# A fused attention and feed-forward kernel: steps dealt 4, 9, 9, 8, value products one tick earlier, and a new order of the tail's transfers

## The chip, the cores and the metric

The kernel runs on one core of a Trainium2 chip, in float32. The metric is the device time of one execution in microseconds (us), lower is better. A core has TensorE (PE, matmuls; PEld is its weight load), VectorE (DVE), ScalarE (ACT), GpSimd (POOL) and SyncE (SP). Each of them works through its own instructions in program order and waits on semaphores. SP and POOL also issue transfers (DMA), each in its own queue, in that order.

## What is computed

A gate per token mixes sliding-window attention and a SwiGLU feed-forward layer. S = 2048 tokens, D = 512, 32 heads of 16, a window of 256, hidden size F = 1792.

```python
def reference(A_x, A_wqkv, A_wo, B_x, B_w_gate, B_w_up, B_w_down, gate_w):
    ...
        mask = (idx[:, None] - idx[None, :] >= 0) & (idx[:, None] - idx[None, :] < W)
        scores = jnp.where(mask[None, None], scores, -1e9)
        p = _softmax(scores, axis=-1)
        o = jnp.einsum("bhqk,bhkd->bhqd", p, v)
        return (lambda x, *d: x.transpose(*d))(o, 0, 2, 1, 3).reshape(B, S, D) @ wo
    ...
        g = _silu(x @ w_gate)
        u = x @ w_up
        return (g * u) @ w_down
    x = A_x
    g = _sigmoid((x * gate_w).sum(-1, keepdims=True))
    a = _A_ref(x, A_wqkv, A_wo)
    b = _B_ref(x, B_w_gate, B_w_up, B_w_down)
    return g * a + (1 - g) * b
```

## The kernel before

Products that need precision are made of three matmuls of halves: a value is split into a high part (a rounding copy, a "cast") and a low part (the difference), and high x high, high x low and low x high are added (`split`, L66 to L71; `mm3`, L80 to L82).

**Prologue** (to about 175 us): values, queries and keys, and the gate and up products of the first two of 14 feed-forward units. Results that are needed later go to DRAM: queries and keys to `xd`, values to `vd`, gate and up products to `raws[unit, gate or up, chunk of 512 tokens]`.

**Attention** (to about 639 us). Heads are handled four at a time: G = 8 groups. A group has 16 blocks of 128 tokens (t counts all 128 blocks), and four blocks make a slot, so a group has four slots. A block has four ticks (`hd`), one per head. In a tick stand:
- `stage1(g + 1, i)`: a score matmul for the next group (L554), whose row maxima DVE takes (L556, the instruction `CUSTOM_DVE_ANT_0`, `ISA` in a listing). It writes PSUM tiles `ps1` (two buffers). There is none for the last group's stretch (t >= 112).
- `stage2(g, i)`: a score matmul with the maximum folded in (L593), its exponential on ACT (L595, into `pt`), and after every second head two triangular selects on POOL (L597, L600). It writes `ps2` (two buffers).
- some *steps* of the feed-forward products: a step is a pair of matmuls on the two halves of the array's rows (L498). A unit has 48 steps; ACT copies its results to `ev` tiles (L525, a ring of five buffers that others use too) and they are written to `raws` (L526).
- `tick_end`, which emits everything that a table by tick number (`AT`, filled by `at`, `later`, `spread`) holds for this tick: loads, weight splits, early tiles.

In the first block of each slot the value products of the slot before are added (`av`, 96 small matmuls, L617): 64 for a group's first chunk. They write one `ps1` and one `ps2` tile (two `ps1` tiles in the last group), which `evacuate` empties: ACT copies `ob` (L628), DVE copies `oe` (L634; L630 in the last group), and the sum goes to `od` (L636). Just ahead of `evacuate` the list `UNDER` is emitted (the gate's row sums, L674). After blocks 7 and 15 of a group `put_max` negates and transposes the maxima of half a group (L567, L568) and sends them to the query tiles.

Steps per block: 7 with value products (2, 1, then the products and one more, then 1, 2), else 7 or 8 (`STEPS` = 60 per 8 blocks). So 30 per slot.

In the last group ACT and DVE prepare the start of the feed-forward tail. `tile_early(n)` makes silu of tile n from an exponential on ACT (L711), an addition, a reciprocal and two products on DVE (L712 to L715), and a cast and difference. `INV[c]` (`invert`) loads the denominators of attention chunk c from `od`, inverts them (L689) and writes them to `rd`.

**Tail.** The hidden tiles (c, n), four chunks of 512 tokens by 14 units, are loaded (`load_kept`, L874, tiles `got`, four buffers), multiplied (`hidden`: silu on ACT, L879, product on DVE, L880), split (`halved`: `hh`, `hl`) and multiplied with w_down (`step`, twelve matmuls per tile). Between them stand the output products of attention per chunk: shares of the attention output and of the inverses are loaded by POOL (`load_oc`, `load_rd`, 256 KB each, in the list `shares_due`), divided on DVE (`attn_divide`), split by ACT and POOL (`attn_split`), multiplied (`attn_out`) and added (`attn_put`). A counter m = 14 c + n numbers the tiles. At the end the sums are stored.

## Time and profile before

| what | value |
| --- | --- |
| median of 3 runs | 849.83 us (849.62 to 850.51) |
| the profiled execution | 850.33 us, its span 848.6 us |
| granted TensorE clock, mean of the span | 0.994 |
| longest idle time of PE | 5.48 us before L80, 2.65 us before L593 |
| mean transfer rate | 187 GB/s |

A row of the timeline gives the start and the length in us, the engine, the line, the operation and the tiles (output <- inputs); in square brackets stands how long the engine sat idle before it and what ended that. A row of the waits gives the total in us, the number of times and the longest. A row of the windows gives busy us and count of instructions of PE, PEld, DVE, ACT and POOL, then the granted clock, the share of the 16 DMA engines, and GB/s. A row of a group ends with busy us, the mean ns of one, and the idle time before.

### The profile page before, as it was taken

Reading aid. Unit: us, or ns where it says so; the run is one execution under the profiler, and the core shown is the slowest. Engines: PE = TensorE matmul, PEld = TensorE weight load, DVE = VectorE, ACT = ScalarE, POOL = GpSimd, SP = SyncE. Lnnn points to the kernel's source line nnn. Section 1 sums busy time; section 2 is a strip of 40 time slices with the busy share of each in tenths; the row PEclk is TensorE's granted clock in tenths of the full one; section 3 lists DMA queues with packets and bytes.
Section 4 is the critical chain, followed back from the end, with each engine's and each line's share of the span. In section 5 each row is a group of like instructions: output and inputs, shape, how many; then the busy total and the mean of one; then the engine's idle time right before and its main releaser. Section 6 shows DMA issues by size and latency. Waiting matters only on the chain. (4 is left out here: it accounts for less than half of the span.)

```text
span 848.6 us, 20406 instructions
## 1 busy us (share of the span) xinstructions
PE 826.2 (97%) x7681; PEld 673.8 (79%) x7681; DVE 555.6 (65%) x1420; ACT 471.5 (56%) x955; POOL 395.6 (47%) x708
## 2 busy tenths in 40 slices
PE   8999999999999999999999999999987999999998
PEld 7888888889877787787887878878765878888886
DVE  5675554158886888878878777775474566365552
ACT  7455553211676777667776767767754553444341
POOL 5124440431565666666665665656743433123120
PEclk9999999999999999999999999999998999999999
DMA  8456666485354465644656445524646998586731
GB/s 297 138 173 223 244 252 224 143 282 181 133 166 137 158 212 162 219 159 152 206 166 219 144 141 168 181 85 146 213 146 225 282 264 267 147 248 196 224 118 50
DMA packets 80418, 158.90 MB, mean 187 GB/s; under 512 B 14912, under 2 KB 19392, under 8 KB 80320
## 3 DMA queue, kind: packets, MB, share of 16 engines
q1 hardware_dynamic: 69552, 129.27, 47.3%
q0 software_dynamic: 10192, 27.29, 10.1%
q8 instruction: 60, 0.98, 0.5%
q10 hardware_dynamic: 576, 1.05, 0.4%
q14 instruction: 38, 0.31, 0.1%
HBM read 92.80 MB, written 64.75 MB: 186 GB/s over the span
## 5 line engine op out<-in xcount | busy, mean ns | idle before, releaser
L556 DVE CUSTOM_DVE_ANT_0 ps<-ps,mask 128x384 f32<-128x384 f32 (+2 forms) x512 | 271.3, 544 | 38.0 <-PE ps L554 19.9
L595 ACT ACTIVATE pt<-ps 128x384 f32<-128x384 f32 (+2 forms) x512 | 236.8, 481 | 59.3 <-PE ps L593 24.3
L593 PE MATMUL ps<-q,k 64*128 64x384 f32 (+2 forms) x512 | 175.8, 352 | 4.7 <-ACT pt L595 4.2
L554 PE MATMUL ps<-k,q 63*128 63x384 f32 (+2 forms) x512 | 162.5, 337 | 0.3
L597 POOL TENSOR_SCALAR_AFFINE_SELECT pt<-pt 128x256 f32<-128x256 f32 x256 | 108.6, 424 | 88.7 <-ACT pt L595 87.2
L554 PEld LDWEIGHTS ps<-k,q 63*128 63x128 f32 x512 | 88.8, 184 | 30.2 <-DVE oe L634 10.2
L593 PEld LDWEIGHTS ps<-q,k 64*128 64x128 f32 x512 | 93.8, 185 | 20.9 <-ACT pt L595 16.8
L600 POOL TENSOR_SCALAR_AFFINE_SELECT pt<-pt 128x256 f32<-128x256 f32 x224 | 93.0, 415 | 0.0
L498 PE MATMUL pa<-xhi,wh 64*128 64x512 f32 x368 | 85.8, 405 | 0.0
L498 PE MATMUL pa<-xhi,wl 64*128 64x512 f32 x368 | 85.7, 398 | 0.0
L498 PE MATMUL pb<-xhi,wh 64*128 64x512 f32 x368 | 85.1, 403 | 0.0
L498 PE MATMUL pa<-xlo,wh 64*128 64x512 f32 x368 | 85.1, 398 | 0.0
L498 PE MATMUL pb<-xhi,wl 64*128 64x512 f32 x368 | 83.7, 394 | 0.0
L498 PE MATMUL pb<-xlo,wh 64*128 64x512 f32 x368 | 83.1, 395 | 0.0
L617 PE MATMUL ps<-pt,vg 64*32 64x320 f32 (+4 forms) x2816 | 76.8, 348 | 4.4 <-POOL pt L597 2.9
L880 DVE TENSOR_TENSOR sg<-got,sg 128x512 f32<-128x512 f32 x52 | 43.8, 843 | 54.5 <-ACT sg L879 38.5
L617 PEld LDWEIGHTS ps<-pt,vg 64*32 64x32 f32 x2816 | 53.2, 106 | 30.0 <-issue 8.3
L556 DVE DVE_READ_ACCUMULATOR2_ANT mx<- 128x1 f32 x512 | 72.1, 141 | 0.0
L635 POOL TENSOR_TENSOR oe<-oe,ob 128x512 f32<-128x512 f32 (+1 forms) x28 | 35.2, 1256 | 55.7 <-ACT ob L628 51.1
L68 ACT CAST hh<-sg 128x512 fp32r<-128x512 f32 x53 | 32.7, 616 | 46.4 <-PE ps L81 34.0
L628 ACT COPY ob<-ps 128x512 f32<-128x512 f32 (+1 forms) x32 | 18.3, 573 | 64.1 <-PE ps L617 64.1
L71 POOL TENSOR_TENSOR ol<-raw,oh 128x512 fp32r<-128x512 f32 x16 | 22.1, 1382 | 67.9 <-ACT oh L68 67.8
(248 smaller groups left out, 1805.3 us busy)
## 6 DMA issues: line engine op xcount, KB each, us to landing
got<-raws SPq DMA_DIRECT2D x104, 256.0 KB
raws<-ev SPq DMA_DIRECT2D x96, 256.0 KB
q<-xd SPq DMA_DIRECT2D x96, 128.0 KB
k<-xd SPq DMA_DIRECT2D x96, 128.0 KB
xd<-cx SPq DMA_DIRECT2D x16, 512.0 KB
xd<-cy SPq DMA_DIRECT2D x16, 512.0 KB
od<-oe POOLq DMA_DIRECT2D x32, 256.0 KB, 3.6
raw<-wgu SPq DMA_DIRECT2D x24, 256.0 KB
```

Of the source, the lines that this page charges most:

```text
L68: nc.scalar.copy(hi, src)
L71: lo_eng.tensor_tensor(out=lo, in0=src, in1=hi.bitcast(F32), op=ALU.subtract)
L498: mm = nc.tensor.matmul(ps[me], w[r], x[r], start=not second and i == 0, stop=bool(second) and i == n - 1)
L554: nc.tensor.matmul(ps[:, :n], QT[g % 2][pr][r, q0:q0 + P], KT[g % 2][pr][r, k0:k0 + n], start=True, stop=True)
L556: mx = nc.vector.tensor_tensor_reduce(out=ps[:, :n], in0=ps[:, :n], in1=mask[:, 3 * P - n:], scale=1.0, scalar=NEG, op0=ALU.add, op1=ALU.m ...
L593: nc.tensor.matmul(ps[:, :n], KT[g % 2][pr][r, k0:k0 + P], QT[g % 2][pr][r, k0:k0 + n], start=True, stop=True)
L595: BEHIND.append(nc.scalar.activation(pt[:, j, :n], ps[:, :n], AF.Exp, scale=SCALE))
L597: nc.gpsimd.affine_select(out=pt[:, :, :P], in_=pt[:, :, :P], pattern=[[0, 2], [1, P]], compare_op=ALU.is_ge, fill=0.0, base=0, channel_mu ...
L600: nc.gpsimd.affine_select(out=pt[:, :, 2 * P:], in_=pt[:, :, 2 * P:], pattern=[[0, 2], [-1, P]], compare_op=ALU.is_ge, fill=0.0, base=-1, ...
L617: nc.tensor.matmul(AV[g, c][h][32 * j:32 * j + 32, q0 - c * CH:q1 - c * CH], VG[4 * g + kb // 4][o, kb % 4, 17 * j:17 * j + 32], PT[g, kb, ...
L635: nc.gpsimd.tensor_tensor(out=e[:, lo:], in0=e[:, lo:], in1=o[:, lo:], op=ALU.add)
L880: nc.vector.tensor_tensor(out=sg, in0=gu[1], in1=sg, op=ALU.mult)
```

## The change

1. *Steps.* The blocks of a slot get 4, 9, 9 and 8 steps (`DEAL`), spread evenly over the ticks. The total stays 30.
2. *Value products* with `UNDER` and `evacuate` stand in the first tick of a slot's first block, before that tick's steps, instead of in the second tick after them. `put_max` goes into `UNDER`.
3. *Early tiles.* The two tiles are worked on in parallel, at other ticks: exponential, then DVE's four instructions at once, then the split nine ticks later. Tile 2's raw data are loaded from the first tick of block 14. Tile 3 is no longer loaded in attention, but as the tail's first `got` tile.
4. *Inverses.* Chunks 0 and 1 are inverted in the last group, with twelve ticks between load and reciprocal; chunks 2 and 3 in the tail, by tiles 6, 8 and 10.
5. *Queues.* The last unit's results and five w_down loads go through POOL's queue instead of SP's.
6. *Tail.* The output weights are loaded at tiles 11 to 14 and split at 13 to 16. Shares start at tile 14, one per tile (before: from tile 4, with gaps later). The output products of the four chunks start at m = 22, 31, 42 and 49 (before: 15, 21, 35 and 49). For chunks 0 to 2 ACT now scales the feed-forward sums into one of two buffers, and DVE adds attention's output and stores; before, this held for chunk 0 alone, and in the others the order was reversed.

```diff
+        DEAL = 4, 9, 9, 8
...
-                n = (2, 1, 1, 2)[hd] if values else (k + 1) * STEPS // 32 - k * STEPS // 32
-                if t < G * NB:
-                    run(steps, n)
-                tick_end()
-                if hd == 1 and values:
+                if hd == 0 and values:
                     av(*divmod(d - 1, NCH))
                     while UNDER:
                         UNDER.pop(0)()
                     evacuate(*divmod(d - 1, NCH))
-                    if t < G * NB:
-                        run(steps, STEPS // 8 - 6)
+                if t < G * NB:
+                    n = DEAL[part]
+                    run(steps, (hd + 1) * n // 4 - hd * n // 4)
+                tick_end()
             if i in (7, 15) and g + 1 < G:
-                put_max(g + 1, i // 8)
+                UNDER.append(lambda g=g, i=i: put_max(g + 1, i // 8))
...
-        early = chain(tile_early(0), tile_early(1))
-        for n in range(12):
-            at(4 * (g7 + 10) + 2 + n + n // 6, lambda: run(early, 1))
-        at(4 * (g7 + 12) + 2, lambda: tile_load(2, RAW_AT[2]))
-        at(4 * (g7 + 14) + 2, lambda: tile_load(3, RAW_AT[3]))
+        for n, ticks in enumerate(((2, 5, 5, 5, 5, 14), (7, 14, 14, 14, 14, 23))):
+            early = tile_early(n)
+            for m in ticks:
+                at(4 * (g7 + 10) + m, lambda early=early: run(early, 1))
+        at(4 * (g7 + 14), lambda: tile_load(2, RAW_AT[2]))
...
-        INV = [invert(c) for c in range(NCH)]
-        for c in range(NCH - 1):
+        INV = [invert(c, osb) for c in range(2)]
+        for c in range(2):
             for n in range(2):
-                at(4 * (g7 + 5 + 4 * c) + 2 + 6 * n, lambda c=c: run(INV[c], 1))
+                at(4 * (g7 + 5 + 4 * c) + 3 + 12 * n, lambda c=c: run(INV[c], 1))
...
-            nc.sync.dma_start(WDRAW[f], wd[f])
+            nc.gpsimd.dma_start(WDRAW[f], wd[f])
...
+                        queue = nc.gpsimd if key == UNITS[-1] else nc.sync
+                        later(4 + m, lambda m=m: queue.dma_start(raws[key[1], key[2], 2 * hf + m], places[m]))
...
         run(last_tile)
-        run(INV[3])
...
+            ga = GA[c % 2][:, b]
+            if c < NCH - 1:
+                nc.vector.scalar_tensor_tensor(ga, pa, gate[:, t:t + 1], ga, op0=ALU.mult, op1=ALU.add)
+                nc.gpsimd.dma_start(out[0, t * P:(t + 1) * P], ga)
...
-        loads = seq[4:]
+        loads = seq[3:]
...
+                if n == 6:
+                    inv = [invert(c3, wop) for c3 in range(2, NCH)]
+                    run(inv[0], 1)
+                if n == 8:
+                    run(inv[0])
+                    run(inv[1], 1)
+                if n == 10:
+                    run(inv[1])
             m = NF * c + n
-            if m >= 4 and (m < 20 or (m % 2 == 0 if m < 36 else m % 3 != 2)) and shares_due:
+            if 11 <= m < 15:
+                ready.append(load_wo(m - 11))
+            if 13 <= m < 17:
+                ready.pop(0)()
+            if m >= 14 and shares_due:
                 shares_due.pop(0)()
-            if c == 1:
-                attn_step(0, n - 1)
-            if c > 1 and n == 0:
-                attn_step(c - 1, 7)
-            if c:
-                attn_step(c, n - 7)
+            for o, at_ in enumerate((22, 31, 42, 49)):
+                attn_step(o, m - at_)
```

Three places in the order of instructions. A listing has line, operation, output <- inputs and shape. Line numbers of the changed kernel differ: L556 becomes L566, L567 and L568 become L577 and L578, L634 becomes L644, L595 becomes L605, L628 becomes L638, L689 becomes L457, L880 becomes L872.

DVE around the second slot's value products of group 0 (t = 8), before: two instructions per max (`ISA`), the negation and transpose of `put_max`, the copy `oe` after the products.

```order
L556 ISA ps_2571,mx<-ps_2571,mask 128x384
L556 ISA mx 128x1
L567 TENSOR_SCALAR mt<-mx 128x32
L568 STREAM_TRANSPOSE mtt<-mt 128x32
L556 ISA ps_2592,mx<-ps_2592,mask 128x384
L556 ISA mx 128x1
L556 ISA ps_2605,mx<-ps_2605,mask 128x384
L556 ISA mx 128x1
L634 COPY oe<-ps_2615 128x512
```

The same place in the changed kernel:

```order
L566 ISA ps_2570,mx<-ps_2570,mask 128x384
L566 ISA mx 128x1
L566 ISA ps_2584,mx<-ps_2584,mask 128x384
L566 ISA mx 128x1
L577 TENSOR_SCALAR mt<-mx 128x32
L578 STREAM_TRANSPOSE mtt<-mt 128x32
L644 COPY oe<-ps_2591 128x512
```

One max instead of two now stands between the block's start and the copy, and the pair stands behind it, next to the products.

ACT in the last group, before: tile 0's exponential (L711, `ev<-k_1521`), its cast (L68), tile 1's exponential, the copy `ob` after value products; the rest are the scores' exponentials.

```order
L711 ACTIVATE ev<-k_1521 128x512
L595 ACTIVATE pt<-ps_9919 128x384
L595 ACTIVATE pt<-ps_9922 128x384
L595 ACTIVATE pt<-ps_9942 128x384
L595 ACTIVATE pt<-ps_9945 128x384
L68 CAST k_1507<-ev 128x512
L595 ACTIVATE pt<-ps_9962 128x384
L595 ACTIVATE pt<-ps_9965 128x384
L711 ACTIVATE ev<-q_1505 128x512
L628 COPY ob<-ps_9979 128x512
```

In the changed kernel, from tile 1's exponential on, which now precedes tile 0's cast:

```order
L711 ACTIVATE ev<-q_1505 128x512
L605 ACTIVATE pt<-ps_9960 128x384
L605 ACTIVATE pt<-ps_9963 128x384
L638 COPY ob<-ps_9969 128x512
L605 ACTIVATE pt<-ps_10028 128x384
L605 ACTIVATE pt<-ps_10031 128x384
L605 ACTIVATE pt<-ps_10043 128x384
L605 ACTIVATE pt<-ps_10046 128x384
L605 ACTIVATE pt<-ps_10060 128x384
L605 ACTIVATE pt<-ps_10063 128x384
L68 CAST k_1507<-ev 128x512
```

Between tile 0's exponential and its cast four scores' exponentials stood; now twelve, tile 1's exponential and `ob` do. Tile 1's cast (not shown) stands behind the last scores' exponential.

DVE at the start of the tail, before: the third and fourth inverse (L689), tile 2's product (L724), the last `oe`, then tile 3's product (L880, `sg<-q_1505`) and w_down's differences.

```order
L689 RECIPROCAL den<-den 128x128
L724 TENSOR_TENSOR ev<-k_1521,ev 128x512
L630 TENSOR_TENSOR oe<-ps_10179,ob 128x512
L71 TENSOR_TENSOR k_1507<-ev,k_1507 128x512
L689 RECIPROCAL den<-den 128x128
L880 TENSOR_TENSOR sg<-q_1505,sg 128x512
L71 TENSOR_TENSOR q_1505<-raw,q_1505 128x512
L880 TENSOR_TENSOR sg<-got_10270,sg 128x512
```

In the changed kernel the inverses of chunks 2 and 3 stand here (L872 is the product, `hl` the low half of a tile):

```order
L457 RECIPROCAL den<-den 128x128
L872 TENSOR_TENSOR sg<-got_10345,sg 128x512
L71 TENSOR_TENSOR hl<-sg,hh 128x512
L872 TENSOR_TENSOR sg<-got_10384,sg 128x512
L71 TENSOR_TENSOR hl<-sg,hh 128x512
L457 RECIPROCAL den<-den 128x128
L872 TENSOR_TENSOR sg<-got_10409,sg 128x512
L71 TENSOR_TENSOR hl<-sg,hh 128x512
```

The third moved from ahead of tile 2's product to behind tile 8's, the fourth from ahead of tile 3's to behind tile 10's.

More of the change, by code (lines that the diff above doesn't have):

```diff
@@ L450, in gated_mix, with invert @@
     WD, GOT = {}, {}
+    shares = od.rearrange("g (j e) s -> (g j) e s", e=32)[:, DH]
+    def invert(c, pool):
+        den = pool.tile([P, P], F32, name="den")
+        nc.gpsimd.dma_start(den, shares[:, c * CH:(c + 1) * CH].rearrange("h (q i) -> h q i", q=4))
+        yield
+        nc.vector.reciprocal(den, den)
+        nc.gpsimd.dma_start(rd[c].rearrange("h (q i) -> (h q) i", q=4), den)
+        yield
     def load_wd(f, piece, raw=None):
@@ L525, in copies @@
                         later(1 + m, lambda m=m: nc.scalar.copy(places[m], ps[m]))
-                        later(4 + m, lambda m=m: nc.sync.dma_start(raws[key[1], key[2], 2 * hf + m], places[m]))
+                        queue = nc.gpsimd if key == UNITS[-1] else nc.sync
+                        later(4 + m, lambda m=m: queue.dma_start(raws[key[1], key[2], 2 * hf + m], places[m]))
                 return copies
@@ L681, in gate_end @@
             nc.vector.tensor_scalar(igate, gate, -1.0, 1.0, op0=ALU.mult, op1=ALU.add)
-        shares = od.rearrange("g (j e) s -> (g j) e s", e=32)[:, DH]
-        def invert(c):
-            den = osb.tile([P, P], F32, name="den")
-            nc.gpsimd.dma_start(den, shares[:, c * CH:(c + 1) * CH].rearrange("h (q i) -> h q i", q=4))
-            yield
-            nc.vector.reciprocal(den, den)
-            nc.gpsimd.dma_start(rd[c].rearrange("h (q i) -> (h q) i", q=4), den)
-            yield
         def wd_early(k, f, piece):
             at(k, lambda: later(4, load_wd(f, pieces[piece], kept())))
-        RAW_AT, TILE_AT = (14, 8, 14, 8), (12, 10, 13)
+        RAW_AT, TILE_AT = (14, 8, 14), (12, 10, 13)
         TILE = [None] * 3
@@ L826, in load_oc @@
             nc.gpsimd.dma_start(OC[c][:, k], heads[:, :DH, c * CH:(c + 1) * CH])
-        RD = [t.bitcast(F32) for c in range(2, 4) for t in (xhi[c], xlo[c])]
+        RD = [t.bitcast(F32) for t in (xhi[2], xlo[2], xhi[3], xhi[2])]
         def load_rd(c, k):
@@ L887, in halved @@
             return c, n, hh, hl
-        ACC, GA = {}, []
+        ACC, GA = {}, [by_k(slot("k11", F32)), const.tile([P, NK, CH], F32, name="xlo3")]
         COLS = slice(0, D // 2), slice(D // 2, D)
@@ L925, in gated_mix @@
         seq = [(c, n) for c in range(NCH) for n in range(NF)]
-        ready = [load_wo(k) for k in range(3)]
-        GOT[0, 3] = GOT[3]
+        ready = []
         shares_due = [lambda f=f, c=c, k=k: f(c, k) for c in range(NCH) for k in range(NK) for f in (load_oc, load_rd)]
-        loads = seq[4:]
+        loads = seq[3:]
         for _ in range(3):
```

23 lines of the change are left out of this document (3 added, 20 removed).

## The prediction

> **What bounds the kernel now.** I read the page's busy times first, then the waits of TensorE (PE), then windows set at the starts of the value products and at the gaps, then the timeline inside the two worst gaps.
>
> ```profile
> PE 826.2 (97%) x7681; PEld 673.8 (79%) x7681; DVE 555.6 (65%) x1420; ACT 471.5 (56%) x955; POOL 395.6 (47%) x708
> ```
>
> PE is the bound, and no part of the change takes a matmul away, so only PE's idle and slow stretches can be won. The waits of PE over the whole run name five:
>
> ```profile
> PE ps L80 <- ACT hh L68: 5.5, 1, 5.5
> PE ps L593 <- ACT pt L595: 4.2, 3, 2.6
> PE ps L617 <- POOL pt L597: 2.9, 4, 0.7
> PE ps L617 <- DVE mx L556: 1.4, 3, 0.5
> PE ps L82 <- DVE hl L71: 1.2, 1, 1.2
> ```
>
> The windows show where they fall (after the engines' busy times stand the granted clock, the DMA share and GB/s):
>
> ```profile
> 490.20:542.10 51.90, 51.39 (x721) 41.69 (x720) 40.08 (x137) 36.14 (x80) 33.65 (x72) 1.00 0.45 147
> 594.50:606.00 11.50, 11.50 (x141) 9.08 (x140) 5.32 (x10) 7.79 (x19) 8.85 (x17) 1.00 0.58 185
> 618.60:636.20 17.60, 13.41 (x165) 10.52 (x164) 12.66 (x11) 9.00 (x23) 7.59 (x17) 0.90 0.49 157
> 626.40:630.10 3.70, 3.70 (x21) 3.70 (x22) 3.63 (x3) 1.74 (x4) 2.42 (x7) 0.54 0.60 224
> 647.20:652.60 5.40, 0.00 (x0) 0.00 (x0) 2.08 (x3) 0.64 (x2) 0.54 (x1) 0.81 0.59 221
> 652.60:657.50 4.90, 4.75 (x11) 3.35 (x12) 4.90 (x10) 4.22 (x8) 4.89 (x9) 0.51 0.66 189
> 657.50:688.50 31.00, 31.00 (x137) 25.32 (x135) 16.19 (x25) 17.20 (x30) 11.67 (x15) 1.00 1.06 279
> 689.80:845.10 155.30, 154.86 (x685) 128.16 (x685) 82.94 (x110) 59.90 (x105) 37.85 (x45) 1.00 0.62 185
> ```
>
> A slot of the last group (four blocks and one set of value products) takes 11.5 us undisturbed and 17.6 us in 618.6 to 636.2, where PE idles 4.2 us and then runs 3.7 us at a granted clock of 0.54. From 647.2 it idles 5.4 us and runs the next 4.9 us at 0.51. From 689.8 to 845.1 nothing is left to win. So the change can win in three places: the transition between attention and the feed-forward tail, the waits before value products, and small waits inside the slots that busy time hides.
>
> **The early tiles (attention's last slot).** The timeline of ACT, DVE and PE ahead of the 2.65 us gap:
>
> ```profile
> 617.54 0.94 DVE L689 RECIPROCAL den<-den 128x128 f32<-128x128 f32 x1
> 618.41 3.29 DVE L713 RECIPROCAL ev<-ev 128x512 f32<-128x512 f32 x1
> 622.46 0.69 DVE L715 TENSOR_TENSOR ev<-k,ev 128x512 f32<-128x512 f32 x1
> 623.18 0.62 ACT L68 CAST k<-ev 128x512 fp32r<-128x512 f32 x1 [5.69 <-DVE ev L715]
> 624.24 0.82 PE L593 MATMUL ps<-q,k 64*128 64x384 f32 x2 [2.65 <-ACT pt L595]
> ```
>
> The cast of tile 0 stands on ACT five ticks after its exponential, with DVE's chain of 3.29 + 2 x 0.69 us and an inverse of 0.94 us between. ACT waits 5.69 us in it, and the exponentials of the scores behind it release PE's score buffers. After the change the cast stands nine ticks after DVE's chain was issued, across a set of value products: nine ticks at 11.5/16 = 0.72 us are 6.5 us, where the chain needs about 5 (an addition, 3.29, and two of 0.69). Tile 1's cast moves behind the last exponential, so that its wait (I estimate about 1 us, since the low half of tile 0 goes ahead of its chain) has only copies and the third tile behind it, and no score buffer hangs on those. Removed: 17.60 - 13.41 = 4.2 us of idle, and of the slow 3.7 us the share 1 - 0.54, 1.7 us. Against it I set 1.0 us for remaining ACT waits, because the last blocks have ever fewer columns and give PE less cover. **Term: -4.9 us.** Bounds: -5.9 (no wait left) and 0 (rival 3). The two inverses of the denominators that stay here each cost DVE 0.94 us beside a free PE: nothing; uncovered, 1.9 us.
>
> **The start of the tail.**
>
> ```profile
> 641.47 4.04 SPq L874 DMA_DIRECT2D got<-raws  x8
> 645.54 0.63 ACT L879 ACTIVATE sg<-got 128x512 f32<-128x512 f32 x1 [4.44 <-DMA got<-raws]
> 645.13 0.54 POOL L687 DMA_DIRECT2D den<-od  x1 [4.17 <-DMA od<-oe]
> 650.43 0.95 DVE L689 RECIPROCAL den<-den 128x128 f32<-128x128 f32 x1 [9.72 <-DMA den<-od]
> 651.30 0.63 DVE L880 TENSOR_TENSOR sg<-q,sg 128x512 f32<-128x512 f32 x1
> 651.96 0.62 ACT L68 CAST hh<-sg 128x512 fp32r<-128x512 f32 x1 [5.79 <-DVE sg L880]
> 652.63 0.80 PE L80 MATMUL ps<-q,hh 128*128 128x512 f32 x1 [5.48 <-ACT hh L68]
> ```
>
> DVE stands 9.72 us in the fourth inverse, whose load had to wait for the last attention output to land; tile 3's product stands behind it, and PE idles 5.48 us. The change moves the inverses of chunks 2 and 3 behind tiles 8 and 10. That removes 5.48 us and the slow stretch after it, 4.9 x (1 - 0.51) = 2.4 us. The 1.23 us before 689.8 (the L82 row of the waits) lies at the end of the 31 us in which DMA was saturated (share 1.06, 279 GB/s); the change takes ten-odd loads of 256 KB out of that stretch, so I count it as removed. Together -9.1 us.
>
> What it adds there: tile 3 is no longer loaded under attention; it is now the first `got` load. Today's first one was issued at 641.47, after SyncE had stood behind unit 13's writes and two w_down loads, which move to POOL's queue; so it should go out when the value products release the memory, 2.8 us earlier against PE. Its tile is needed three tiles after them. A tile is twelve matmuls of 0.227 us (31.00/137 in the saturated window), 2.7 us, so 8.2 us after. The load lands 4.1 us after issue (641.47 to 645.54), the next pair about 2 us later at 279 GB/s (512 KB), and silu 0.63, product 0.63, cast 0.62 and low half 0.7 follow, part of them behind the next tile's silu: 7 to 8.5 us. It is a close fit. A second close fit is the fourth inverse: its load goes out only after the third's store, and DVE may stand some 3 us in it, but DVE is then up to three tiles (8.2 us) ahead. A third: from tile 14 one share of 256 KB is issued per tile beside 512 KB of `got`, 768 KB in 2.7 us or 289 GB/s, over the 279 measured, for the eleven tiles before output products stretch the steps: 31.0 us of transfers in 29.9 us of PE, plus four weights of 256 KB; four buffers of lead hide most of it. For the three I set 2.0 us. **Term: -7.1 us**, bounds -9.1 and 0.
>
> POOL's queue takes nine more transfers of 256 KB at 0.54 us each (the 645.13 row), 5 us of POOL, which is 47% busy and whose selects for the last products are already ahead of most of them: nothing; if they stood ahead of all, the last value products would wait at most 1.6 us for the three that come early. The evacuation of chunks 1 and 2 goes from DVE to ACT, four of about 0.63 us, 2.5 us per chunk boundary on an engine that is busy 59.90 of the last 155.30 us: nothing; uncovered, 2 x 2.5 us.
>
> **The maxima (put_max).** Timeline of DVE, with PE's next value product:
>
> ```profile
> 397.00 0.37 DVE L567 TENSOR_SCALAR mt<-mx 128x32 fp32r<-128x32 f32 x1
> 397.41 0.21 DVE L568 STREAM_TRANSPOSE mtt<-mt 128x32 f32<-128x32 f32 x1
> 397.55 0.53 DVE L556 CUSTOM_DVE_ANT_0 ps<-ps,mask 128x384 f32<-128x384 f32 x1
> 398.28 0.51 PE L617 MATMUL ps<-pt,vg 64*32 64x320 f32 x8 [0.46 <-DVE mx L556]
> 398.50 0.92 DVE L674 SCALAR_TENSOR_TENSOR xn<-xn,gwb 128x512 f32<-128x512 f32 x1
> 400.90 0.69 DVE L634 COPY oe<-ps 128x512 f32<-128x512 f32 x1 [1.47 <-issue]
> 401.51 0.56 DVE L556 CUSTOM_DVE_ANT_0 ps<-ps,mask 128x384 f32<-128x384 f32 x1
> ```
>
> Negation and transpose hold the next block's first max back, and the value product waits for the buffer which that max frees. The seven waits of L617 in the list above are this pattern: 2.9 + 1.4 = 4.3 us. Under the product DVE has 1.47 us idle, and the pair needs about 0.6 to 0.9: covered. **Term: -4.3 us**, bounds -4.3 and 0 (the wait moves to the copy behind it).
>
> **The deal.** PE's work per slot is the same: 30 steps, 16 pairs of score matmuls, one set of value products. The rows that give their pace:
>
> ```profile
> 402.57 0.40 PE L498 MATMUL pb<-xlo,wh 64*128 64x512 f32 x2
> 402.80 0.40 PE L498 MATMUL pb<-xhi,wl 64*128 64x512 f32 x2
> 403.04 0.34 PE L554 MATMUL ps<-k,q 63*128 63x384 f32 x1
> 403.21 0.40 PE L498 MATMUL pb<-xhi,wh 64*128 64x512 f32 x2
> 411.69 2.56 PE L617 MATMUL ps<-pt,vg 64*32 64x320 f32 x96
> ```
>
> A step is 0.23 us, a pair of scores 0.17, the products 2.5: 30 x 0.23 + 16 x 0.17 + 2.5 = 12.1 us, against 51.9/4 = 13.0 per slot, so about 0.9 us per slot is lost in short waits. In the three blocks without products PE now has 23 steps (7.3 us); a tick is about 0.6 us, and two buffers ask for one max (0.34 of matmul, 0.57 of max) per two ticks, so they lose little. With 26 steps (8.0 us) they should lose less: I take 0.2 us per slot of gain. In the block with products the steps fall from 7 to 4. The products now follow the first scores directly: the last max before them ends 0.34 + 0.57 after its scores began, and PE is there after two steps and a pair, 0.17 + 0.46 + 0.17 = 0.80, so it waits 0.1 to 0.2. After them PE has a single step per tick (0.40 us) where copy and maxes follow each other at 0.6: by the order of 400.90 and 401.51 the third and fourth scores and the next block's first wait some 0.45 us together, against 0.15 to 0.3 today. Gain and loss are equal to a tenth. **Term: 0**, bounds over 28 slots -5.6 (0.2 each, no new wait) and +8.4 (0.3 each).
>
> **Sum.** -4.9 - 7.1 - 4.3 + 0 = -16.3 us. The profiled execution's span is 848.6 us, its own time 850.33, the median of the runs 849.83: the median lies 1.2 above the span. 848.6 - 16.3 + 1.2 = 833.5.
>
> The slow clock is a term that rests on a row: 0.54 came after an idle time of 2.65 us. [...]
>
> **Rivals.**
> 1. *The first tiles come late.* If tile 3's load takes the place of the inverse (landings 2 us apart and the next tile's silu ahead of its cast), PE idles some 3 us and the clock falls again for 2.4 us, and tile 4 and 5 wait 1 to 2 us more: +6, 839.5. For it: the saturated DMA rows; against: SyncE's queue is free.
> 2. *The deal's wait decides, and the kernel is slower.* The products now begin 0.8 us closer to the last exponentials, and need the selects of the last block near their end:
>
> ```profile
> PEld ps L617 <- POOL pt L597: 6.4, 11, 1.1
> ```
>
>    This wait exists already, up to 1.1 us. If every slot had it, the 28 slots would cost 28 x 1.1 = 31 us, and with it 864. It decides from 16.3/28 = 0.58 us per slot. Against it: the last block's probabilities are used in the products' last third, 1.7 us after their start.
> 3. *The change doesn't do what it says for the early tiles:* the cast still stands on DVE, the 2.65 us gap and its slow clock stay: +4.9, 838.4.
> 4. *Better:* the deal also wins its 5.6 and the three close fits cost nothing: 833.5 - 5.6 - 3 = 825.
>
> **How the numbers follow.** Forecast (829 to 837) 0.54; rival 1 0.15; rival 2 0.16, of which 0.04 lies below today's time (a wait of 0.2 to 0.5 per slot, 839 to 848); rival 3 0.05; rival 4 0.10. About 0.2% (1.7 us) is what a measurement of this kernel tells from no change. Slower by more than that is rival 2 beyond 0.64 us per slot, 0.09; within it, 0.03; faster 0.88. The range from 825 to 845 leaves out the far half of rival 2 and a corner of rival 4.
>
> **What would show it.** Right: no PE gap over 1.5 us between 600 and 690, granted clock 1.00 there, the last three slots of attention each 11 to 12 us, no wait of ACT for L715's successor over 2 us, DVE's waits for `den` without PE idle behind them, and four slots of a group in 51 to 52 us. Wrong in the deal: a group of over 52.5 us, with PE's waits at the first or the last value products. Wrong in the tail: a PE wait on `hh` or `hl` of tiles 3 to 6 or at tiles 20 to 25. The whole is wrong if rival 2's wait stands in most slots.

## The result, and the profile after

The changed kernel takes 847.52 us (median of 19 runs, 844.67 to 849.72); the kernel before took 849.83 in 19 runs beside it (848.55 to 853.08). The ratio is 0.9968, interval 0.9958 to 0.9978. It is faster, but by 2.3 us where 16.3 were forecast, and outside the range. The profiled execution has a span of 846.7 us and a time of its own of 848.42. One execution of e5 below, 1310 us at a granted clock of 0.56, is left out of its times and ratio.

The busy times of the changed kernel, and its list of PE's waits (who was waited for, total us, times, longest):

```profile
PE 829.8 (98%) x7681; PEld 680.0 (80%) x7681; DVE 558.7 (66%) x1420; ACT 472.6 (56%) x955; POOL 400.3 (47%) x717
```

```profile
PE ps L82 <- DVE hl L71: 4.4, 3, 3.6
PE ps L627 <- DVE mx L566: 1.5, 9, 0.2
PE ps L603 <- ACT pt L605: 1.4, 4, 0.7
...
PE ps L80 <- ACT ob L638: 0.9, 1, 0.9
```

Four of the five waits that the prediction named went down: 5.5 us on `hh` (gone), 4.2 on the exponentials (now 1.4), and the two ahead of the value products, 4.3 together (now 1.5). The fifth, on `hl`, went up from 1.2 to 4.4 us. Together they fall from 15.2 to 7.3 us. Yet PE's busy time rose from 826.2 to 829.8 us with the same 7681 matmuls. Time that vanished as waits came back inside "busy", where a list of waits doesn't show it.

To see where, cut the run at the start of the last stage-1 score and at the start and end of the last group's value products. The rows of the line of the stage-1 scores give the first (shortest, median and longest duration in ns, then first and last start in us): L554 of the kernel before, and the same line of the changed kernel:

```profile
L554 PE MATMUL ps<-k,q x512: 219/337/447, 172.6 to 580.1; 63*128 63x384 f32 x150, 63*128 63x128 f32 x11, 63*128 63x256 f32 x10
```

```profile
L564 PE MATMUL ps<-k,q x512: 218/337/447, 172.7 to 585.3; 63*128 63x384 f32 x150, 63*128 63x128 f32 x11, 63*128 63x256 f32 x10
```

The scores start together and end 5.2 us later than before: a stretch that was forecast to shrink by 4.3 us (the maxima) grew. Worked out from the starts and ends of single rows:

| stage (us) | before | forecast | changed | e1 | e9 |
|---|---|---|---|---|---|
| first score of group 1 to the last stage-1 score | 364.3 | 360.0 | 369.4 | 359.1 | 359.1 |
| last group: from its first value products (those of the group before) to the end of its last | 56.9 | 52.0 | 51.9 | 50.4 | 50.3 |
| tail: from there to the end | 209.9 | 202.8 | 208.4 | 205.2 | 202.7 |
| span | 848.6 | 832.3 | 846.7 | 832.0 | 829.4 |

(The rest of a span is some 216 us ahead of the first stage, and 1.1 to 1.8 between the first and the second.) e1 and e9 are kernels of the experiments. Three stages, three answers: the stage of the early tiles came out as forecast, the tail won 1.4 us of 7.1, and the body of attention lost 5.1 us where it should have won 4.3. One caution on the second row: the change moves the products one tick forward, and with them the start of this stage. From the last stage-1 score to the end of the last products it is 58.7 us before, 53.0 in the changed kernel and 52.2 in e1.

Windows of the changed kernel at the last group, and at the one large gap in the tail:

```profile
586.40:638.30 51.90, 50.46 (x752) 39.70 (x751) 26.41 (x37) 35.63 (x84) 34.64 (x76) 1.00 0.54 175
676.50:680.10 3.60, 0.05 (x1) 0.05 (x1) 3.60 (x2) 0.70 (x2) 3.48 (x4) 1.00 0.68 211
681.50:684.90 3.40, 3.40 (x9) 2.62 (x9) 0.12 (x1) 2.52 (x5) 0.00 (x0) 0.50 0.52 154
```

The last line of the three comes behind the one above it: 1.45 us after PE's 3.58 us of idle time, which end at 680.05, the granted clock falls to 0.50 for 3.4 us.

The timelines of DVE, POOL and ACT of the changed kernel ahead of that gap tell what PE waited for:

```profile
665.88 0.95 DVE L457 RECIPROCAL den<-den 128x128 f32<-128x128 f32 x1 [5.51 <-DMA den<-od]
...
674.61 1.36 DVE L872 TENSOR_TENSOR sg<-got,sg 128x512 f32<-128x512 f32 x1 [4.23 <-ACT sg L871]
675.90 4.10 DVE L71 TENSOR_TENSOR hl<-sg,hh 128x512 fp32r<-128x512 f32 x1
...
661.16 0.54 POOL L455 DMA_DIRECT2D den<-od  x1 [2.30 <-DMA rd<-den]
667.12 0.54 POOL L458 DMA_DIRECT2D rd<-den  x1 [5.42 <-DVE den L457]
667.66 1.60 POOL L811 DMA_DIRECT2D raw<-wo  x3
674.13 1.30 POOL L71 TENSOR_TENSOR wol<-raw,woh 128x512 fp32r<-128x512 f32 x1 [4.87 <-ACT woh L68]
...
676.30 1.27 POOL L71 TENSOR_TENSOR wol<-raw,woh 128x512 fp32r<-128x512 f32 x1
677.51 0.63 POOL L823 DMA_DIRECT2D xhi<-od  x1
678.17 1.27 POOL L71 TENSOR_TENSOR wol<-raw,woh 128x512 fp32r<-128x512 f32 x1
...
673.42 0.62 ACT L68 CAST woh<-raw 128x512 fp32r<-128x512 f32 x1 [4.14 <-DMA got<-raws]
```

Read it from the top. The fourth inverse's load goes out at 661.16, when the third's store has landed, because both use the one `den` buffer. DVE stands 5.51 us for it. POOL stands behind DVE, for the store at 667.12, and the three loads of `wo` are queued behind that store. ACT comes to the first cast of `wo` (L68, `woh`) and stands 4.14 us; the profile names a tile's load (`got`), but the first `wo` load landed at 673.28, 5.6 us after its issue and just before the cast. When it ends, POOL makes its low halves one after the other, and in their midst DVE's `hl`, which takes 0.68 us elsewhere, takes 4.10. PE's tile waits for that `hl`. So PE idles some 10 us after the inverse, through five links. Two of them are read from the order in the queues, and the experiments below test the first and the last.

### The profile page after: what moved, and what is told of

Read it like the earlier page. It is cut to its first block, busy times and chain, and to the rows that moved or that the text cites. A ratio compares the mean times of both kernels' runs of the same rounds, so it can differ in the third digit from the quotient of the medians.

```text
span 846.7 us, 20416 instructions
## 1 busy us (share of the span) xinstructions
PE 829.8 (98%) x7681; PEld 680.0 (80%) x7681; DVE 558.7 (66%) x1420; ACT 472.6 (56%) x955; POOL 400.3 (47%) x717
## 4 chain that ended last, share of the span: by engine, by line
PE 85%; DMA 6%; DVE 3%; ACT 2%; POOL 1%; issue 1%; SPq 0%; DVEq 0%; ACTq 0%
PE pb L507 14%; PE pa L507 14%; PE ps L627 9%; PE ps L564 7%; PE ps L380 6%; PE ps L603 5%; PE pb L380 4%; PE pa L380 4%; PE ps L82 4%; PE ps L81 4%; PE ps L80 4%; PE ps L211 3%; DMA got<-raws 2%; PE pb L81 2%; PE pb L80 2%; DMA xhi<-rd 2%
## 5 line engine op out<-in xcount | busy, mean ns | idle before, releaser
L566 DVE CUSTOM_DVE_ANT_0 ps<-ps,mask 128x384 f32<-128x384 f32 (+2 forms) x512 | 272.7, 544 | 50.5 <-PE ps L564 28.6
L605 ACT ACTIVATE pt<-ps 128x384 f32<-128x384 f32 (+2 forms) x512 | 236.0, 479 | 67.1 <-PE ps L603 30.0
L603 PE MATMUL ps<-q,k 64*128 64x384 f32 (+2 forms) x512 | 173.8, 349 | 2.2 <-ACT pt L605 1.4
L607 POOL TENSOR_SCALAR_AFFINE_SELECT pt<-pt 128x256 f32<-128x256 f32 x256 | 106.1, 416 | 73.6 <-ACT pt L605 73.1
L627 PE MATMUL ps<-pt,vg 64*32 64x320 f32 (+4 forms) x2816 | 78.7, 348 | 3.0 <-DVE mx L566 1.5
L627 PEld LDWEIGHTS ps<-pt,vg 64*32 64x32 f32 x2816 | 56.7, 106 | 25.6 <-issue 10.2
L872 DVE TENSOR_TENSOR sg<-got,sg 128x512 f32<-128x512 f32 x53 | 43.4, 818 | 45.3 <-ACT sg L871 36.6
L566 DVE DVE_READ_ACCUMULATOR2_ANT mx<- 128x1 f32 x512 | 72.4, 141 | 0.0
L68 ACT CAST hh<-sg 128x512 fp32r<-128x512 f32 x53 | 32.6, 615 | 43.6 <-PE ps L81 38.2
L71 DVE TENSOR_TENSOR hl<-sg,hh 128x512 fp32r<-128x512 f32 x53 | 40.6, 766 | 22.9 <-ACT hh L68 22.9
L71 POOL TENSOR_TENSOR ol<-raw,oh 128x512 fp32r<-128x512 f32 x16 | 25.3, 1578 | 60.2 <-ACT oh L68 60.2
```

Of the source, the lines that this page charges most:

```text
L71: lo_eng.tensor_tensor(out=lo, in0=src, in1=hi.bitcast(F32), op=ALU.subtract)
L566: mx = nc.vector.tensor_tensor_reduce(out=ps[:, :n], in0=ps[:, :n], in1=mask[:, 3 * P - n:], scale=1.0, scalar=NEG, op0=ALU.add, op1=ALU.m ...
L603: nc.tensor.matmul(ps[:, :n], KT[g % 2][pr][r, k0:k0 + P], QT[g % 2][pr][r, k0:k0 + n], start=True, stop=True)
L605: BEHIND.append(nc.scalar.activation(pt[:, j, :n], ps[:, :n], AF.Exp, scale=SCALE))
L607: nc.gpsimd.affine_select(out=pt[:, :, :P], in_=pt[:, :, :P], pattern=[[0, 2], [1, P]], compare_op=ALU.is_ge, fill=0.0, base=0, channel_mu ...
L627: nc.tensor.matmul(AV[g, c][h][32 * j:32 * j + 32, q0 - c * CH:q1 - c * CH], VG[4 * g + kb // 4][o, kb % 4, 17 * j:17 * j + 32], PT[g, kb, ...
```

## The experiments

Ratios are to the kernel before, run beside it on the same chip. Two things have to be told apart: which of three edits lengthened the body (the deal, the place of the products, the maxima under them), and which link of the chain in the tail decides.

**e1, e2, e3: the deal and the place, one by one.** e1 puts both back as they were and keeps all else; e2 keeps the new deal with the products behind the second scores; e3 keeps the products behind the first scores with the old steps. e1's edit:

```diff
-                if hd == 0 and values:
+                n = (2, 1, 1, 2)[hd] if values else (k + 1) * 60 // 32 - k * 60 // 32
+                if t < G * NB:
+                    run(steps, n)
+                tick_end()
+                if hd == 1 and values:
                     av(*divmod(d - 1, NCH))
...
                     evacuate(*divmod(d - 1, NCH))
-                if t < G * NB:
-                    n = DEAL[part]
-                    run(steps, (hd + 1) * n // 4 - hd * n // 4)
-                tick_end()
+                    if t < G * NB:
+                        run(steps, 1)
```

e2 only moves the block with `av` and `evacuate` behind `tick_end()` with `hd == 1`; e3 only takes e1's `n` in place of DEAL, with the extra step at the end of the second tick.

> The changed kernel with the steps and the place of the value products as before (7, then 8, 7, 8 or 7, 8; products in the second tick), and put_max still under the products. The body of attention is read from the start of the last of the 512 stage-1 scores: 580.1 us before, 585.3 us in the changed kernel. Theory A (the deal and the place together cost the body some 9 us, and put_max under the products wins its 4.3 us): 575.8 us, and the whole 838 us. Rival B (put_max under the products wins nothing, since its wait only moves behind the copy of the products): 580 us, 842 us. Rival C (the body's loss comes from transfers or from elsewhere in the change): 585 us and no change of time.

> The changed kernel with the products back in the second tick after its steps, but the steps dealt 4, 9, 9, 8. If the short deal costs (one step per tick in the block with products, so that scores wait in turn for copy and maxima), the last stage-1 score starts at 583 us or later, and the kernel takes 845 us or more. If the place costs (products that begin before the last tick's maximum, exponential and selects are done), it starts at 576 to 578 us, and the kernel takes about 839 us.

> The changed kernel with the products in the first tick as in the change, but seven steps in that block (2, 2, 1, 2 after the products) and 8, 7, 8 or 7, 8 in the others. If the place costs: last stage-1 score at 583 us or later, 845 us or more. If the short deal costs: 576 to 578 us, about 839 us. If both are needed for the loss, this and the kernel with the new deal and the late products both stand near 580 us.

| | time, us | ratio | last score starts | block with products | second | third | fourth | slot |
|---|---|---|---|---|---|---|---|---|
| before | 849.46 | 1 | 580.1 | 5.41 | 2.54 | 2.60 | 2.56 | 13.11 |
| e1: old steps, old place | 833.84 | 0.982 [0.9802, 0.9839] | 574.5 | 5.24 | 2.55 | 2.59 | 2.56 | 12.93 |
| e2: new deal | 842.12 | 0.9916 [0.9897, 0.9935] | 582.1 | 4.97 | 2.86 | 2.79 | 2.58 | 13.20 |
| e3: new place | 840.04 | 0.9884 [0.9863, 0.9905] | 578.8 | 5.33 | 2.58 | 2.61 | 2.57 | 13.09 |
| changed: both | 847.52 | 0.9968 [0.9958, 0.9978] | 585.3 | 4.97 | 2.94 | 2.82 | 2.58 | 13.31 |

(The last five columns are the mean lengths of the four blocks of a slot, from score row to score row, over groups 1 to 5.) The deal alone ends attention's scores 7.6 us later than e1, the place alone 4.3, both 10.8. Up to 0.5 us of that lies ahead of group 1's first score, where these kernels do not differ; counted from there it is 7.4, 4.1 and 10.3. So each costs by itself, and the two nearly add up; of the expected cases the last of e3's (both kernels near 580 us) is the nearest. e1 is some 4 us faster than expected; its scores end 1.3 us earlier, and its tail takes 205.2 us instead of 208.4 (its fourth inverse stood 1.27 us). Rival B of e1, that the maxima under the products win nothing, is refuted: they stand there in e1 too, and its body is the shortest of the five.

The table also says how. A step is 0.23 us of PE. The deal takes three steps out of the block with products, 0.70 us, and that block gets 0.27 shorter. The three arrive in the second and third block, which had 8 and 7 and now have 9 each, and these get 0.31 + 0.20 = 0.51 us longer. Where steps arrive, most of their price is paid; where they left, a wait takes most of their room. Most of this wait is hidden from the list of PE's waits (6.5 us on `oe` stand there in e2, none in e1, e3 and the changed kernel), since a matmul's record (0.34 to 0.40 us) is longer than the 0.17 to 0.23 us after which the next one starts in the prediction's rows (402.57 to 402.80, 403.04 to 403.21). The waits of the weight loads (PEld), which stand ahead of the matmuls (in the changed kernel the last one starts at 585.1 us, its matmul at 585.3), show it. Between 216 and 574 us, e1:

```profile
PEld ps L564 <- DVE oe L644: 10.2, 27, 0.4
...
PEld ps L564 <- DVE mx L566: 6.5, 31, 0.3
PEld ps L627 <- issue: 4.5, 16, 0.3
```

e2, the new deal in the old place:

```profile
PEld ps L564 <- DVE oe L644: 16.2, 26, 0.7
PEld ps L564 <- DVE mx L566: 11.7, 58, 0.4
PEld ps L627 <- POOL pt L607: 6.3, 17, 0.5
```

e3, the old steps in the new place:

```profile
PEld ps L564 <- DVE mx L566: 12.8, 63, 0.3
PEld ps L627 <- issue: 9.6, 24, 0.5
```

In e2 no step is left between the products and the next scores, which need the buffer that DVE's copy `oe` frees: the waits for it grow from 0.38 us each (27 of them) to 0.62 (26). The new place trades this wait for more, shorter ones on the maxima (31 waits become 63) and a later start of the products. These waits can't be added up to the loss, because part of each lies beside the matmul ahead (over the changed kernel's span PEld is busy 80% and PE 98%).

PE's timeline of one such block in the changed kernel, and DVE's beside it:

```profile
453.38 2.55 PE L627 MATMUL ps<-pt,vg 64*32 64x320 f32 x96
455.87 0.50 PE L507 MATMUL pb<-xhi,wh 64*128 64x512 f32 x2
...
456.76 0.44 PE L564 MATMUL ps<-k,q 63*128 63x384 f32 x1
...
457.29 0.44 PE L564 MATMUL ps<-k,q 63*128 63x384 f32 x1
...
457.92 0.44 PE L564 MATMUL ps<-k,q 63*128 63x384 f32 x1
...
456.01 0.69 DVE L644 COPY oe<-ps 128x512 f32<-128x512 f32 x1 [0.77 <-PE ps L627]
456.62 0.56 DVE L566 CUSTOM_DVE_ANT_0 ps<-ps,mask 128x384 f32<-128x384 f32 x1
...
457.24 0.57 DVE L566 CUSTOM_DVE_ANT_0 ps<-ps,mask 128x384 f32<-128x384 f32 x1
...
457.76 0.57 DVE L566 CUSTOM_DVE_ANT_0 ps<-ps,mask 128x384 f32<-128x384 f32 x1
```

After the products scores start every 0.53 to 0.63 us, at the pace of copy and maxima on DVE; with one step per tick PE has 0.23 + 0.17 = 0.40 us of work in between. That is the floor of the block: fewer steps there leave holes.

**e6: the gentlest deal.** On e5 (below), steps 6, 8, 8, 8 with the products behind the second scores, to see whether a flat deal wins where 4, 9, 9, 8 loses.

```diff
-                n = (2, 1, 1, 2)[hd] if values else (k + 1) * 60 // 32 - k * 60 // 32
+                n = (2, 1, 1, 2)[hd] if part == 0 else 2
...
-                    if t < G * NB:
-                        run(steps, 1)
```

> The same with the steps dealt 6, 8, 8, 8, products in the second tick. Theory (the block with products takes what DVE and ACT need, some 4.9 to 5 us, however few steps it has; a block with 8 steps is already paced by PE, and only blocks with 7 lose): the block with products falls from 5.24 to about 5.1 us, the others stand at 2.57, a slot wins 0.1 us, the last stage-1 score starts 3 us earlier, near 571.5 us, and the kernel takes about 3 us less than the one with the old deal. Rival (every step taken out of that block costs): the last score starts at 574 us or later.

It takes 832.47 us, ratio 0.9797 [0.9777, 0.9818], where e5 beside it has 0.9792; its last score starts at 575.7, and its blocks are 5.22, 2.54, 2.63 and 2.55. The expected 3 us are not there: the rival's sign (574 us or later) came. The step more in the third block costs 0.04 us, so there was room; but the step less in the block with products saves only 0.02. It is the one right behind the products, and the wait on the copy shows it (weight loads of e6, same stretch):

```profile
PEld ps L564 <- DVE oe L644: 16.3, 27, 0.7
```

So the block with products stands close to its floor with 7 steps already (a step less saves 0.02 us of 0.23, three less in e2 0.27 of 0.70), and neither deal beats e1's 12.93 us per slot.

**e7: the maxima alone.** e1 with put_max called where the kernel before calls it:

```diff
-                UNDER.append(lambda g=g, i=i: put_max(g + 1, i // 8))
+                put_max(g + 1, i // 8)
```

> The kernel with the old deal and place (833.8 us, last stage-1 score at 574.5 us), with put_max back ahead of the next block's maxima. Theory (its negation and transpose hold the products' buffer): seven gaps of PE of 0.4 to 0.7 us ahead of value products return, last score at 579 to 580 us, 838 to 839 us. Rival (the gain of that kernel over the first came from elsewhere): last score at 575 us and no change of time.

840.84 us, 0.9901 [0.9877, 0.9924]. The last score starts at 580.1, 5.6 us after e1's as the theory had it, and the wait list has the old pattern back:

```profile
PE ps L627 <- POOL pt L607: 2.9, 4, 0.7
...
PE ps L627 <- DVE mx L566: 1.4, 3, 0.5
```

Those are the seven waits of the prediction to the digit, and the blocks are those of the kernel before (5.41, 2.54, 2.60, 2.56). From group 1's first score on, the maxima are worth 5.2 us (364.3 against 359.1). The time is 2 us over what was expected, because 2.6 us of e7's longer span are in the tail: its fourth inverse stood 4.48 us (1.27 in e1) and a `hl` took 4.1 us, although the tail's code is the same. In e3 a `hl` took 4.1 us too, and in e1 the longest took 2.3. So the collision depends on how the engines stand to each other when the tail begins; what shifts them was not looked for.

**e4: a second den buffer.** The changed kernel with two buffers and both inverses' loads issued together, at tile 6 (the two edits were not tried apart):

```diff
-    def invert(c, pool):
-        den = pool.tile([P, P], F32, name="den")
+    def invert(c, pool, n=1):
+        den = pool.tile([P, P], F32, name="den", bufs=n)
...
-                    inv = [invert(c3, wop) for c3 in range(2, NCH)]
+                    inv = [invert(c3, wop, 2) for c3 in range(2, NCH)]
...
+                    run(inv[1], 1)
...
-                    run(inv[1], 1)
```

> The changed kernel with two buffers for the denominators of chunks 2 and 3 and both loads issued at tile 6. In the changed kernel DVE stands 5.51 us in the fourth inverse; POOL issues the output weights only behind its store, ACT stands 4.14 us in their cast, DVE's low half takes 4.10 us beside two low halves of weights on POOL, PE idles 3.58 us and runs 4.9 us at a granted clock of 0.65. Theory A (the late inverse starts that chain): the wait of DVE falls under 1 us, the PE gap goes with its slow clock, 5 to 6 us less, 842 us. Rival B (the low halves of the output weights on POOL hold DVE wherever they stand): the inverse's wait goes, a DVE instruction of 3 us or more beside them stays, and PE keeps a gap over 2 us: at most 1 us less.

842.08 us, 0.9909 [0.9892, 0.9925]; the tail takes 202.2 us, 6.3 less than in the changed kernel and 7.7 less than before. That is the expected 5 to 6 us and a little more. DVE's inverses now wait for nothing, and a window on the place of the old gap is full:

```profile
657.27 0.94 DVE L457 RECIPROCAL den<-den 128x128 f32<-128x128 f32 x1
...
660.48 0.95 DVE L457 RECIPROCAL den<-den 128x128 f32<-128x128 f32 x1
```

```profile
660.00:690.00 30.00, 30.00 (x134) 24.85 (x133) 17.26 (x24) 16.89 (x30) 13.78 (x19) 1.00 0.84 250
```

**e8: the last link alone.** The changed kernel with the low halves of `wo` on DVE; the single `den` buffer stays.

```diff
-            return lambda: split(woh[:, k], wol[:, k], raw, *act)
+            return lambda: split(woh[:, k], wol[:, k], raw, nc.scalar, nc.vector)
```

> The changed kernel with the low halves of the output weights on DVE instead of POOL. In the changed kernel DVE's low half of a tile takes 4.10 us where others take 0.68, beside two of POOL's low halves and two of its transfers; PE idles 3.58 us behind it. Theory A (POOL at work on SBUF holds DVE's instruction): no low half over 1.5 us at tiles 13 to 16, the gap of 3.58 us falls under 1.5 us, 3 to 5 us less, though the inverse's wait of 5.5 us stays. Theory B (the late inverse alone took DVE's lead): the gap stays over 2.5 us.

844.44 us in its one run, span 842.7, tail 204.6; a single run, so its time is only an indication. DVE's queue of e8:

```profile
665.13 0.95 DVE L457 RECIPROCAL den<-den 128x128 f32<-128x128 f32 x1 [4.95 <-DMA den<-od]
...
675.86 0.68 DVE L71 TENSOR_TENSOR hl<-sg,hh 128x512 fp32r<-128x512 f32 x1
676.47 0.68 DVE L71 TENSOR_TENSOR wol<-raw,woh 128x512 fp32r<-128x512 f32 x1
```

The inverse still stands 4.95 us, and yet the gap at 676 is gone: no `hl` from 660 to 684 us takes more than 0.69 us. Of the 6.3 us that the chain costs, 3.8 hang on its last link, by this run. Part of the rest stands in new gaps of 0.27, 1.13 and 0.61 us between 692 and 700, the three waits of this row of e8:

```profile
PE ps L82 <- DVE hl L71: 2.0, 3, 1.1
```

**e5 and e9: the best parts together.** One wait is left between attention and the tail of e1: PE waits 2.18 us for the last `ob` there, 0.89 in the changed kernel. ACT's queue of e1 around it:

```profile
626.48 0.62 ACT L68 CAST q<-ev 128x512 fp32r<-128x512 f32 x1 [2.80 <-DVE ev L715]
627.11 1.28 ACT L723 ACT_TABLE_LOAD   x1
628.41 0.63 ACT L723 ACTIVATE ev<-k 128x512 f32<-128x512 f32 x1
628.94 1.05 ACT L534 COPY ev<-pb 128x512 f32<-128x512 f32 x2
629.89 0.60 ACT L638 COPY ob<-ps 128x512 f32<-128x512 f32 x1
```

The cast of tile 1 stands 2.80 us, and `ob` behind it frees a `ps` buffer that PE's first tile waits for (the 2.18 us). e5 is e1 with e4's pair of buffers and this cast behind `ob`; e9 is the same kernel once more, and the readings below are of its trace.

```diff
-        for n, ticks in enumerate(((2, 5, 5, 5, 5, 14), (7, 14, 14, 14, 14, 23))):
+        for n, ticks in enumerate(((2, 5, 5, 5, 5, 14), (7, 14, 14, 14, 14, 26))):
```

> The kernel with the old deal and place and put_max under the products (833.8 us), with both denominator loads issued together, and the cast of early tile 1 moved behind the copy ob of the last value products. There ACT stood 2.80 us in that cast ahead of ob, PE idled 2.18 us for ob and ran 3.4 us at a granted clock of 0.50. Theory: that gap, its 1.7 us of slow clock and the inverse's wait of 1.27 us go, and with them most of the gap of 0.72 us: 829 to 830 us. Rival: the table load and silu of tile 2, which stay ahead of ob, keep PE waiting over 1 us: 832 us.

> The kernel of e5 once more (old steps, products behind the second scores, maxima under them, two den buffers, tile 1's cast behind ob), for a profile of it. Theory: 831 to 832.5 us, last scores of attention starting near 574.5, no idle time of TensorE over 1.3 us between 625 and 720 and the granted clock 1.0 there, tail (end of the last value products to the end) near 202.5. Rival: taking tile 1's cast back only moves the wait to a later tile: an idle time of 2 us or more stands at 628 to 645 as in e1, and the time is over 833.

e5 gave a ratio of 0.9792 [0.9774, 0.9809] (three runs, 830.71 to 832.22, all above what was expected), e9 a median of 830.05 us (829.69 to 832.59) and 0.9771 [0.9747, 0.9795], 1 us under what was expected of it. e5's times alone would have spoken for its rival (832 us); e9's trace shows that the rival's wait of PE, over 1 us for `ob`, is not there. The busy times of e9 and its largest wait of PE:

```profile
PE 821.0 (99%) x7681; PEld 667.6 (80%) x7681; DVE 555.7 (67%) x1420; ACT 471.8 (57%) x955; POOL 403.2 (49%) x717
```

```profile
PE ps L82 <- DVE hl L71: 1.5, 2, 1.4
```

Its last score starts at 574.6. PE's busy time is down to 821.0 us for the same 7681 matmuls, the wait on `ob` is gone, the tail takes 202.7 us, and one gap over 0.4 us is left after attention, 1.37 at 689.5 (no more than 1.3 was expected). It is another wait: DVE's division of attention's output, ahead of that `hl`, stood 6.42 us for a share to land. This kernel is faster than the one before and than the changed one.

**e10: e9 with e8's edit.**

> e9 with the low halves of the output weights on VectorE instead of GpSimd, as in e8. If GpSimd's two low halves in a row cost TensorE time here too, 829.5 to 831, some 1 us under e9. Rival: with both den buffers VectorE is ahead enough to take a long low half without TensorE feeling it, and the four halves added to VectorE's queue cost as much as they save: within 0.7 us of e9, either way.

830.37 us, 0.9767 [0.9742, 0.9791]: no different from e9. The rival holds. With both buffers the low halves of `wo` on GpSimd (657 to 663 us in e9) meet no `hl` that PE waits for.

## Why the prediction was wrong, step by step

- **The early tiles, -4.9.** Right in kind, and the fit of the number (5.0 in the table) is partly luck. In e1, with the old deal and place, the stretch from the last stage-1 score on is 6.5 us shorter than before, beyond the bound of 5.9; in the changed kernel the deal and the place take 0.8 of that back, and the rest is the shifted start of the stage. One sentence behind the term was wrong, that behind tile 1's cast "no score buffer hangs on those": `ob` frees a `ps` buffer that the first tile waits for. The cast waited 2.39 us for an estimated 1. PE paid 0.89 us for it, counted in the tail, and in e1 2.18 us, with a granted clock of 0.50 for 3.4 us after it.
- **The start of the tail, -7.1.** The bound of 0 was nearer (-1.4). The pieces named as close fits were looked at one by one: the first `got` load was in time, and the shares cost 0.37 us (DVE stood 3.54 us for one at 704.9). The 279 GB/s that the third close fit took for the most that the transfers move was no ceiling: from 638.3 to 660.0 the changed kernel moves 334 GB/s. The fourth inverse was the one that failed, and not as feared. DVE's stand (5.51 us for an estimated 3) was covered but for 0.50 us, as the text said. What it left out is who else stands behind that wait: POOL's store, behind it POOL's `wo` loads, behind these a cast on ACT. The mechanism that should win was right and its size nearly so: with the second buffer the tail wins 7.7 us.
- **The maxima, -4.3.** Right in kind, 5.2 in size (e7 against e1), beyond the bound of 4.3. The seven visible waits are the 4.3; the other 0.9 us were not looked for further.
- **The deal and the place, 0.** This is the step that failed, by 10.3 us in the body and 0.8 in the last group (e1 against the changed kernel). With the 5.7 missing in the tail, and less the 0.9 and 1.6 that the maxima and the early tiles won beyond their terms, that is 14.3 of the 14.4 us by which the span missed. The sentence is "Gain and loss are equal to a tenth." The gain of 0.2 us per slot in the blocks without products was right: three steps arrive for 0.51 us instead of 0.70. The loss was not: three steps leave the block with products and 0.43 of their 0.70 us stay behind as waits, and the new place costs a further 0.11. The prediction's own rows gave 0.1 to 0.2 ahead of the products and 0.15 to 0.3 more behind them, against a gain of 0.2, so 0.05 to 0.3 per slot; it took the end of that range which is nearest to nothing. Measured are 0.38 per slot (13.31 against 12.93), above even its bound of 0.3.
- **The rivals.** What came is nearest to the second, which named the deal as what decides: 0.38 us per slot, below the 0.58 from which it turns the sign. Its chance was set too low (0.04 for "a wait of 0.2 to 0.5 per slot", 839 to 848 us; 847.5 lies in that band, the tail's loss included). And its mechanism is not what was measured: the weight loads wait 6.3 us for the last probabilities (L607) in e2, but only 0.4 in the changed kernel, where they wait 9.7 us for the copy and 9.6 for the maxima on DVE (e1: 2.2, 10.2 and 6.5). The wait that came is the one that the deal's own term had counted and balanced away.
- **What would show it.** "A group of over 52.5 us, with PE's waits at the first or the last value products" is what the profile has: groups of 53.1 to 53.5 us from score to score, and nine waits of L627 on the maxima. As a sign it was set too near: the kernel before has 52.3 to 52.6 by the same measure. The sign for the tail looked at tiles 3 to 6 and 20 to 25; the gap of 3.58 us came between them, where `wo` is split. That the kernel would be faster (0.88) was right.

## What to carry to other kernels

Before steps are moved out of a loop's slow block to the fast ones, work out the floor that the other engines set in each: here the work left the one block where it filled a wait, and arrived in blocks that had no room. Small waits can hide in an engine's busy time, as here, where a matmul's record of 0.34 to 0.40 us covers the next one's start 0.17 to 0.23 us later; the waits of the weight loads, and the distance from start to start, showed them. When a wait looks covered on its own engine, follow every queue that stands behind the waiting instruction, DMA queues too, up to the engine that counts.

## What the hardware showed that was not expected

A low half on DVE, 0.68 us elsewhere, took 4.10 us beside low halves of 1.27 us each on POOL (676.30 and 678.17). With POOL's halves moved away (e8) it takes 0.68 again (its row at 675.86). In the changed kernel it began at 675.90, between the first of POOL's halves (674.13 plus 1.30) and the second, and ended at 680.00, behind the third (678.17 plus 1.27). Why it takes that long beside them, no run here settles.

The halved clock (0.50) lasted 3.4 us after the gaps of 3.58 us (changed kernel, 681.5 to 684.9) and 2.18 (e1, 631.3 to 634.7). In the kernel before it lasted 3.4 us (626.7 to 630.1) after the gap of 2.65, and 6.8 us (650.6 to 657.4) with the gap of 5.48, the first 2.0 of them still within the gap. Windows of e1 and, for a gap of the same length, of e7:

```profile
628.36:630.54 2.18, 0.00 (x1) 0.00 (x1) 0.72 (x2) 2.17 (x6) 0.00 (x0) 1.00 0.74 206
...
630.54:634.70 4.16, 4.16 (x11) 3.24 (x12) 4.16 (x7) 3.89 (x8) 3.19 (x6) 0.59 0.93 310
```

```profile
633.86:636.04 2.18, 0.00 (x1) 0.00 (x1) 0.71 (x2) 2.17 (x6) 0.00 (x0) 1.00 0.59 217
636.04:640.00 3.96, 3.96 (x17) 3.19 (x18) 3.96 (x7) 3.48 (x7) 2.99 (x6) 1.00 0.87 294
```

After the same 2.18 us of idle time the clock was halved once (e1) and stayed at 1.00 once (e7, to 640.00). So the length of a gap does not decide by itself, and the prediction's price for the slow clock holds for the gaps it read, not for every gap. What else decides, no run here shows.
